# A four-layer decode kernel: two heads' output weights parked in PSUM, parts of two heads of V kept, three units of V read in short transfers

## The chip, the cores and the metric

The kernel runs on 1 core of one Trainium2 chip. Its time is the device time of one execution in microseconds (us), of which the median over several runs is compared. The profile is of one further execution.

## What is computed

Four layers follow each other, attention, a gated block, the same attention again, the same gated block again. The batch is 4 rows with one new position each, the width D is 512, there are 32 query heads over 8 key/value heads of 128, and of the cached 8192 positions the last W = 2048 are attended to.

```python
def _A_ref(x, k_cache, v_cache, wq, wo):
    W = min(4096, max(256, Sk // 4))
    q = (x @ wq).reshape(B, Sq, Hq, Dh).transpose(0, 2, 1, 3)
    k = jnp.repeat(k_cache[:, :, Sk - W:, :], rep, axis=1)
    v = jnp.repeat(v_cache[:, :, Sk - W:, :], rep, axis=1)
    p = softmax(einsum("bhqd,bhkd->bhqk", q, k) * Dh ** -0.5)
    o = einsum("bhqk,bhkd->bhqd", p, v)
    return o.transpose(0, 2, 1, 3).reshape(B, Sq, Hq * Dh) @ wo
def _B_ref(x, w_gate, w_up, w_down):
    return (sigmoid(x @ w_gate) * (x @ w_up)) @ w_down
x = A_x
x = x + _A_ref(_layernorm(x), A_k_cache, A_v_cache, A_wq, A_wo)
x = x + _B_ref(_layernorm(x), B_w_gate, B_w_up, B_w_down)
x = x + _A_ref(_layernorm(x), A_k_cache, A_v_cache, A_wq, A_wo)
x = x + _B_ref(_layernorm(x), B_w_gate, B_w_up, B_w_down)
```

Both attentions use the same K, V, wq and wo, and both gated blocks the same three weights. K and V are 16.8 MB each for the 2048 positions, wq and wo 4.2 MB each, and w_gate, w_up and w_down 1.8 MB each.

## The kernel before

**Storage.** SBUF is cut into units of 256 bf16 columns over 128 partitions, 64 KB each. A head of K or V for the four batch rows is 32 units (2 MB). `kt` has 256 units: all of K, which stays there turned by TensorE from the first attention until the second has used it. `wo_sb` has 64 units, all of wo. `arena` has 75 units, `side` 31; `pt` and `pb` hold weights of the softmax. `WHERE` (lines 426 to 442) names for each load the tensor, the first unit and the number of units. V does not fit beside K, so it is read twice, once in each attention. Half of w_up and w_gate and about half of wq stay from their first use to their second.

**The order of instructions.** Every step is recorded as an operation of a planner with an engine, a planned duration and the blocks and PSUM banks it reads and writes. `_schedule` (line 95) lays the operations out on the engines in advance; `_assign_sync` (line 185) puts the semaphore waits in. All loads but that of x stand on the SyncE queue (SP), strictly in the order in which the program records them: a load that waits until its place is free holds back every load behind it.

**The stages.** First attention: `k_head` turns a head of K (lines 715 to 740), `scores` makes the scores of a head (the matmuls have line 751), the row maximum, the exponential and its transpose; `weights` spreads the result into `pt`; `pv_wo` multiplies by V (line 841 in the wide form, line 883 in the narrow one), scales, and adds the head's share of wo (line 934 for the first seven heads, line 904 for the last). The first gated block is `glu(1, False)`: normalisation, w_up and w_gate (line 1023), w_down (line 1095). `project_q` makes q for the second attention (line 688) from wq, part kept and part loaded as "q01", then subtracts the mean (line 709) and writes `qs` (line 700). The second attention runs the same steps on the K that is still there. V of heads 0 and 1 goes to places in `arena` and `side`; V of heads 2 to 7 goes over K in `kt` as soon as the scores that read that K are done (the load of head h waits for the scores of head h-2). The last gated block is `glu(3, True)`, with w_down in line 1092 and the output copied in line 1105. For the last heads of the second attention `v2_head` (lines 1196 to 1216) adds order edges by hand.

**PSUM.** Eight banks of 2 KB per partition. Banks 0 to 2 take the transposes of K in the first attention, bank 3 its scores, bank 4 sums, banks 5 and 6 the projections and products with V, bank 7 the sum over wo. In the second attention the scores alternate between banks 3 and 0, the turned weights between 1 and 2. `glu` uses banks 0, 1 and 2.

Of the kernel before, what the change touches and what calls it, by code (L numbers as in the profile page):

```python
# [6 lines left out]
BF16 = mybir.dt.bfloat16  # L7
ACTF = mybir.ActivationFunctionType
# [6 lines left out]
class _Op:  # L15
    __slots__ = ("idx", "eng", "name", "dur", "emit", "deps", "odeps", "users", "start", "finish",
                 "sem", "val", "inc", "dma_bytes", "dma_rate", "waits", "prio", "ndeps_left")

    def __init__(self, idx, eng, name, dur, emit):
# [12 lines left out]
        self.inc = 1  # L32
        self.dma_bytes = 0
# [151 lines left out]
def _assign_sync(ops, order, n_dma_sems):  # L185
    counts = {}
    dma_i = 0
    for e in ENGINES:
        for o in order[e]:
            if o.sem is not None:  # L190
                sem = o.sem
            elif e == "sync":
                sem = ("dma", dma_i % n_dma_sems)
                dma_i += 1
                o.inc = 16
            else:
                sem = ("eng", e)
                o.inc = 1
            o.sem = sem
            counts[sem] = counts.get(sem, 0) + o.inc  # L200
            o.val = counts[sem]
# [66 lines left out]
def build(nc, A_x, A_k, A_v, A_wq, A_wo, B_wg, B_wu, B_wd, out):  # L268
# [37 lines left out]
    WIDE = {0: {0: 4, 1: 4, 2: 4, 3: 4, 4: 4, 5: 4, 6: 2}, 2: {2: 2, 3: 2, 4: 2, 5: 2}}  # L306
    HEADS1 = list(range(HKV))
# [29 lines left out]
    with es:  # L337
# [24 lines left out]
        rz = sb("rz", [128, NPT * NR], F32)  # L362
# [40 lines left out]
        def blk_ap(s):  # L403
            return {"kt": kt, "ar": arena, "pt": pt, "pb": pb, "sx": side}[s[0]][:, s[1] * UNIT:(s[1] + s[2]) * UNIT]
# [22 lines left out]
        for h in range(HKV - 1):  # L427
            WHERE["V0_%d" % h] = [ar(MAIN - UHEAD if h % 2 == 0 else 0, UHEAD)]
        WHERE["V0_%d" % (HKV - 1)] = [ar(0, 16), ar(16, 8), ar(24, 8)]
        WHERE["u01"], WHERE["g01"] = ar(MAIN - 2 * GU, 2 * GU), ar(MAIN - 4 * GU, 2 * GU)  # L430
        WHERE.update({
            "g23_1": ar(32, 2 * GU), "u23_1": ar(0, 2 * GU),
            "d0_1": ar(14, 8), "d4_1": ar(22, 8), "d8_1": ar(32, 4), "d10_1": ("pb", 0, 4), "d12_1": ("pt", 4, 4),
            "q01": [ar(36, 10), ar(0, 14), ar(14, 8)],
            "V2_0": [ar(22, 14), sx(0, 8), sx(8, 8), sx(16, 2)],
            "V2_1": [sx(18, NS - 18), ar(0, UHEAD - NS + 18)],
            "g23_3": ar(22, 2 * GU), "u23_3": sx(0, 2 * GU),
            "d0_3": ar(0, 8), "d4_3": ar(8, 8), "d8_3": ar(38, 8), "d12_3": sx(14, 4),
        })
        for h in range(2, HKV):  # L440
            WHERE["V2_%d" % h] = [("kt", (h - 2) * UHEAD + u, n)
                                  for u, n in (((0, 16), (16, 8), (24, 8)) if h == HKV - 1 else ((0, UHEAD),))]
# [20 lines left out]
        def load_v(L, h):  # L463

            got = []
            u0 = 0
            for s in WHERE["V%d_%d" % (L, h)]:
                n = s[2]
                dma("V%d_%d_%d" % (L, h, u0), blk_ap(s), v_d[h][:, :, u0 * UNIT:(u0 + n) * UNIT], w=blk_tok(s),
                    rate={32: "bw_16k", 16: "bw_8k"}.get(n, "bw_4k"), nbytes=128 * n * UNIT * 2)  # L470
                got.append((s, u0 * UNIT // 128))
# [206 lines left out]
        def project_q(L, pieces, pieces_last):  # L678
            if not L:
                return project_first(pieces, pieces_last)  # L680
            prev = []
            toks = []
            wid = NB
            for n, (ap, tk, ktc, q0, q1) in enumerate(pieces):
                def e_q(pe, ap=ap, ktc=ktc, q0=q0, q1=q1, st=(n == 0), last_ktc=pieces_last):
                    last = None
                    for q in range(q0, q1):
                        last = pe.matmul(ps[:, QB, q * wid:(q + 1) * wid],
                                         ap[:, (q - q0) * 128:(q - q0 + 1) * 128],
                                         xn[:, ktc * (NB + 1):ktc * (NB + 1) + wid],  # L690
                                         start=(st and q == q0), stop=(ktc == last_ktc),
                                         skip_group_check=True)
                    return last
                prev = [P.op("tensor", "qproj%d_%d" % (L, n), tm["pe_pair"] * (q1 - q0), e_q,
                             r=list(tk) + [("xn",)], w=[("psq", n)], banks=(QB,), order=prev)]
                toks.append(("psq", n))

            def scaled(src, r, banks):
                P.op("vector", "q_evac%d" % L, c_dve(HQ * NB),
                     lambda v: v.tensor_tensor(  # L700
                         qs[:, 28:28 + HKV * NB * STRIP].rearrange("p (h b s) -> p h b s", h=HKV, b=NB)[:, :, :, 0:REP],
                         src.rearrange("p (h r b) -> p h b r", h=HKV, r=REP)[:, :, 0:NB, :],
                         rstd[:, :].unsqueeze(1).unsqueeze(3).broadcast_to([128, HKV, NB, REP]),
                         ALU.mult),
                     r=r + [("rstd",)], w=[("qs",)], banks=banks)
            if True:
                mc = means(L, tq, cs_q, HQ)
                P.op("vector", "q_mean%d" % L, c_dve(HQ * NB),
                     lambda v: v.tensor_tensor(tq[:, :], ps[:, QB, 0:HQ * NB], tq[:, :], ALU.subtract),
                     r=toks + [mc], w=[mc], banks=(QB,))  # L710
                scaled(tq[:, :], [mc], ())
# [30 lines left out]
        def scores(L, n, h, sbk, tbk):  # L742
# [14 lines left out]
            P.op("tensor", "S%d_%d" % (L, h), 16 * tm["pe_s"] * (0.55 if L == 0 else 1.0), e_s, r=kr + [("qs",)], w=[("pss", sbk)], banks=(sbk,))  # L757
# [32 lines left out]

        def weights(L, n, h, tbk):

            k2 = n % 2
            kp = n % NPT
            ptv = pt[:, kp * NJ4 * NR:(kp + 1) * NJ4 * NR]
            pk = blk_tok(("pt", kp * NR // 4, NR // 4))
# [31 lines left out]
        def wide_pv(L, n, h, wide, bank, out, s):  # L828

            kp = n % NPT  # L830
# [4 lines left out]
            def e_pv(pe):  # L835
                last = None
                for i, (tv, q, c) in enumerate(steps):
                    w0 = (kp * NJ4 + (tv * NB + q) * NCH + c) * NR
# [455 lines left out]
```

## Time and profile before

| what | us |
|---|---|
| median of 3 runs (176.66 to 177.33) | 177.1 |
| the profiled execution, device time | 177.11 |
| its span in the profile | 175.4 |
| TensorE busy in the span | 137.2 |
| VectorE busy | 97.1 |
| ScalarE busy | 71.4 |
| first attention (first instruction to its last wo matmul, line 904) | 0 to 105.6 |
| first gated block, and q | 105.6 to 124.7 |
| second attention (first score matmul to line 904) | 124.7 to 165.1 |
| last gated block | 165.1 to 172.9 |
| output | 172.9 to 175.4 |

The loads move 70.31 MB in 62 transfers, on average 401 GB/s over the span. A busy share of an engine is an average over stages; what a change in a stage is worth shows in which wait of that stage ends last. The times of stages are read from the timeline and the chain of waits. Besides the times of instructions the trace holds a completion record: a wide transfer is shared out to the core's 16 DMA engines, and each adds to the transfer's semaphore when its share has landed, so that a transfer has a first and a last landing.

### The profile page before, as it was taken

Reading aid. Unit: us, or ns where it says so; the run is one execution under the profiler, and the core shown is the slowest. Engines: PE = TensorE matmul, PEld = TensorE weight load, DVE = VectorE, ACT = ScalarE, POOL = GpSimd, SP = SyncE. Lnnn points to the kernel's source line nnn. Section 1 sums busy time; section 2 is a strip of 40 time slices with the busy share of each in tenths; the row PEclk is TensorE's granted clock in tenths of the full one; section 3 lists DMA queues with packets and bytes.
Section 4 is the critical chain, followed back from the end, with each engine's and each line's share of the span. In section 5 each row is a group of like instructions: output and inputs, shape, how many; then the busy total and the mean of one; then the engine's idle time right before and its main releaser. Section 6 shows DMA issues by size and latency. Waiting matters only on the chain.

```text
span 175.4 us, 4862 instructions
## 1 busy us (share of the span) xinstructions
PE 137.2 (78%) x2175; PEld 101.4 (58%) x2175; DVE 97.1 (55%) x240; ACT 71.4 (41%) x125; POOL 6.8 (4%) x17
## 2 busy tenths in 40 slices
PE   0395699898998879988978877449769985978794
PEld 0392488656575657565654567438317753557693
DVE  7444015977848575795884432104298977372440
ACT  2064217848377728384472140300045644341400
POOL 5200000000000000000000002002000000000020
PEclk9999656999999978999999655555586999696858
DMA  5999999999999999999999999999999999999970
GB/s 192 419 424 419 432 441 419 426 419 428 422 419 437 404 441 434 417 426 404 441 422 390 403 420 417 396 403 421 402 427 435 424 426 422 434 405 414 416 285 14
DMA packets 9216, 70.31 MB, mean 401 GB/s; under 512 B 1000, under 2 KB 1772, under 8 KB 5996
## 3 DMA queue, kind: packets, MB, share of 16 engines
q1 hardware_dynamic: 9188, 70.00, 96.1%
q8 instruction: 17, 0.28, 0.6%
q14 instruction: 3, 0.02, 0.0%
q10 hardware_dynamic: 8, 0.00, 0.0%
HBM read 70.00 MB, written 0.00 MB: 399 GB/s over the span
## 4 chain that ended last, share of the span: by engine, by line
DMA 65%; PE 25%; DVE 5%; SPq 2%; ACT 1%; issue 1%; DVEq 0%; ACTq 0%
DMA arena<-in_A_v_cache_dram 31%; DMA kt<-in_A_k_cache_dram 12%; DMA kt<-in_A_v_cache_dram 11%; DMA arena<-in_B_w_down_dram 6%; PE ps L751 5%; DMA arena<-in_A_wq_dram 4%; PE ps L841 4%; PE ps L728 4%; PE ps L883 3%; PE ps L1023 2%; SPq L456 2%; PE ps L821 1%; PE ps L1092 1%; ACT pb L773 1%; DVE nmz L760 1%
## 5 line engine op out<-in xcount | busy, mean ns | idle before, releaser
L738 ACT COPY kt<-ps 128x1024 bf16<-128x1024 bf16 x40 | 39.1, 1017 | 28.0 <-PE ps L728 27.9
L728 PE MATMUL ps<-ident_r,kt 128*128 128x128 bf16 x512 | 40.2, 238 | 5.1 <-DMA kt<-in_A_k_cache_dram 3.2
L728 PEld LDWEIGHTS ps<-ident_r,kt 128*128 128x128 bf16 x512 | 34.7, 109 | 11.9 <-issue 4.4
L738 DVE COPY kt<-ps 128x1024 bf16<-128x1024 bf16 x24 | 29.2, 1215 | 14.1 <-PE ps L728 13.9
L751 PE MATMUL ps<-kt,qs 128*32 128x512 bf16 x256 | 19.2, 429 | 2.5 <-ACT pb L773 1.7
L773 ACT ACTIVATE pb<-ps,nmz 128x512 bf16<-128x512 f32 x16 | 11.1, 691 | 23.6 <-DVE nmz L770 22.1
L806 DVE TENSOR_TENSOR pt<-ps,ofbr 128x1024 bf16<-128x1024 f32 (+1 forms) x16 | 16.2, 1013 | 2.9 <-PE ps L784 2.9
L841 PE MATMUL ps<-arena,pt 128*64 128x512 bf16 (+1 forms) x128 | 13.2, 384 | 3.3 <-DMA arena<-in_A_v_cache_dram 3.3
L760 DVE TENSOR_REDUCE nmz<-ps 128x1 f32<-128x512 f32 x16 | 11.0, 686 | 6.7 <-PE ps L751 6.7
L779 DVE STREAM_TRANSPOSE pb<-pb 128x512 bf16<-128x512 bf16 x16 | 11.2, 700 | 5.1 <-ACT pb L773 5.1
L751 PEld LDWEIGHTS ps<-kt,qs 128*32 128x32 bf16 x256 | 6.0, 103 | 9.8 <-ACT pb L773 2.7
L813 ACT ACTIVATE pt<-ps,ofbr 128x96 bf16<-128x96 f32 x32 | 8.3, 343 | 8.0 <-PE ps L784 8.0
L841 PEld LDWEIGHTS ps<-arena,pt 128*64 128x64 bf16 (+1 forms) x128 | 6.0, 114 | 8.4 <-DMA arena<-in_A_v_cache_dram 4.3
L1023 PE MATMUL ps<-xn,arena 128*128 128x5 bf16 (+1 forms) x196 | 7.4, 172 | 2.6 <-DMA arena<-in_B_w_up_dram 1.1
L1023 PEld LDWEIGHTS ps<-xn,arena 128*128 128x128 bf16 x196 | 7.2, 117 | 2.9 <-DMA arena<-in_B_w_up_dram 1.2
L849 ACT COPY arena<-ps 128x512 f32<-128x512 f32 (+1 forms) x7 | 3.9, 556 | 12.1 <-PE ps L841 12.0
L621 POOL TENSOR_TENSOR rs<-pt,rs 128x4 f32<-128x4 f32 x4 | 4.1, 1014 | 119.7 <-DVE pt L617 119.7
L821 PE MATMUL ps<-rowf,nmz 128*128 128x16 f32 x32 | 7.4, 309 | 1.3 <-DVE pt L806 1.0
L821 PEld LDWEIGHTS ps<-rowf,nmz 128*128 128x128 f32 x32 | 6.0, 233 | 4.1 <-DVE pt L806 1.8
L856 PEld LDWEIGHTS ps<-arena 128*128 128x128 f32 x52 | 6.7, 201 | 2.1 <-ACT arena L849 1.6
L856 PE MATMUL ps<-arena 128*128 128x16 f32 x52 | 7.4, 273 | 0.7
L934 PE MATMUL ps<-wo_sb,onr 128*16 128x512 bf16 x56 | 6.0, 419 | 1.1 <-DVE onr L926 1.1
(127 smaller groups left out, 144.3 us busy)
## 6 DMA issues: line engine op xcount, KB each, us to landing
kt<-in_A_k_cache_dram SPq DMA_DIRECT2D x8, 2048.0 KB, 24.6
arena<-in_A_v_cache_dram SPq DMA_DIRECT2D x7, 2048.0 KB, 20.2
kt<-in_A_v_cache_dram SPq DMA_DIRECT2D x5, 2048.0 KB, 18.5
wo_sb<-in_A_wo_dram SPq DMA_DIRECT2D x8, 512.0 KB, 25.2
arena<-in_B_w_gate_dram SPq DMA_DIRECT2D x3, 896.0 KB, 9.7
arena<-in_B_w_down_dram SPq DMA_DIRECT2D x5, 512.0 KB, 21.6
kt<-in_A_wq_dram SPq DMA_DIRECT2D x1, 2048.0 KB, 11.7
side<-in_A_wq_dram SPq DMA_DIRECT2D x1, 1984.0 KB, 15.9
```

Of the source, the lines that this page charges most:

```text
L728: last = pe.transpose(bankb(bank)[:, (v * NB + q) * 128:(v * NB + q + 1) * 128], kt[:, c0:c0 + 128], ident_b[:, :])
L738: return (e.tensor_copy if ev == "vector" else e.copy)(to, fr)
L751: last = pe.matmul(ps[32 * b:32 * b + 32, sbk, 0:CB * 128], qs[:, q0:q0 + 32], blk_ap(kblk(h, b))[:, c * CB * 128:(c + 1) * CB * 128], sta ...
L760: lambda v: v.tensor_reduce(nmv, ps[:, sbk, 0:CB * 128], AXX, ALU.max, negate=True),
L773: o = a.activation(pbuf[:, :], ps[:, sbk, 0:CB * 128], ACTF.Exp, bias=gv, scale=1.0, accum_out=zv)
L779: P.op("vector", "ptr%d_%d" % (L, h), 650.0, lambda v: v.transpose(turned[:, :], pbuf[:, :]), r=[("pb", 0), ("pb", 1)], w=[("pb", 2), ("pb ...
L806: lambda v: v.tensor_tensor(pv4[:, 0:nj], spread(tbk, nj).unsqueeze(2).broadcast_to([128, nj, NB, REP]), ofb[:, :].unsqueeze(1).unsqueeze( ...
L813: last = a.mul(pv4[:, nj:NJ4, b, :], spread(MB, NJ4 - nj), ofb[:, b:b + 1])
L821: lambda pe: pe.matmul(ps[:, tbk, CB * NQ:CB * NQ + NR], zv.broadcast_to([128, 128]), rowf[:, :], start=True, stop=True),
L841: last = pe.matmul(ps[rows * g:rows * (g + 1), bank, 0:wide * 128].rearrange("p (c d) -> p c d", c=wide), pt[:, w0:w0 + rows], v, start=(i ...
L856: last = pe.matmul(ps[:, out[0], out[1]:out[1] + NR], part[:, c * 128:(c + 1) * 128], ey[wide][:, c * NR:(c + 1) * NR], start=(c == 0), st ...
L1023: last = pe.matmul(ps[:, bank, fc * wid:(fc + 1) * wid], cols[:, fc - g0, :], xn[:, ktc * (NB + 1):ktc * (NB + 1) + wid], start=(ktc == 0 ...
```

## The change

It consists of these parts.

- After the first attention, VectorE copies the output weights of heads 0 and 1 (16 units, 2 MB) bit by bit into PSUM banks 0 to 3 (`stash`), so that 16 units of `wo_sb` are free. During the first gated block and the projection of q they take loads; ScalarE copies the weights back before the second attention uses them. `glu(1)` uses banks 5, 6 and 4 in place of 0, 1 and 2.
- The last 8 units of V of head 6 (in `arena` at 66) and of head 7 (at 24) stay from the first attention; `VKEEP` leaves out their second load. 16 units, 1.05 MB, are not read again. The products with the kept units are made first.
- Many places move. V of head 1 ends and V of heads 2 to 5 starts three units later in `kt`, so that the load of head h now waits for the scores of head h-1. The parts of w_down in the first gated block come in another order.
- `FEW`: the last 2 units of V of head 1 in the first attention, and the last unit of V of head 2 in the second, are loaded by eight transfers each over 16 partitions, which stand ahead of the rest of that head in the queue. On the HBM side each takes 4 positions by 4 batch rows.
- `project_q` puts the first 16 query heads into bank 5 and the others into bank 6, and writes `qs` in two halves: the scores of heads 0 to 3 wait for the first half alone.
- The last head's softmax weights get a third buffer (`PT3`) and its product with V another bank; the hand-made order edges of `v2_head` are gone, and some planned durations differ.

```diff
+    VKEEP = {6: 24, 7: 24}
+    FEW = {(0, 1): 2, (2, 2): 1}
...
-        WHERE["u01"], WHERE["g01"] = ar(MAIN - 2 * GU, 2 * GU), ar(MAIN - 4 * GU, 2 * GU)
+        WHERE["u01"], WHERE["g01"] = ar(52, 2 * GU), ar(38, 2 * GU)
+        PT3 = ar(32, 4)
         WHERE.update({
-            "g23_1": ar(32, 2 * GU), "u23_1": ar(0, 2 * GU),
-            "d0_1": ar(14, 8), "d4_1": ar(22, 8), "d8_1": ar(32, 4), "d10_1": ("pb", 0, 4), "d12_1": ("pt", 4, 4),
-            "q01": [ar(36, 10), ar(0, 14), ar(14, 8)],
-            "V2_0": [ar(22, 14), sx(0, 8), sx(8, 8), sx(16, 2)],
-            "V2_1": [sx(18, NS - 18), ar(0, UHEAD - NS + 18)],
-            "g23_3": ar(22, 2 * GU), "u23_3": sx(0, 2 * GU),
-            "d0_3": ar(0, 8), "d4_3": ar(8, 8), "d8_3": ar(38, 8), "d12_3": sx(14, 4),
+            "g23_1": ("ws", 0, 2 * GU), "u23_1": ar(0, 2 * GU),
+            "d0_1": ar(14, 8), "d4_1": ("ws", 0, 8), "d8_1": ar(32, 4), "d10_1": ("pb", 0, 4), "d12_1": ("pt", 4, 4),
+            "q01": [ar(0, 14), ar(14, 10), ("ws", 8, 8)],
+            "V2_0": [ar(32, 6), sx(0, 16), sx(16, 10)],
+            "V2_1": [sx(26, NS - 26), ar(0, 24), ("kt", 0, 3)],
+            "g23_3": ar(0, 2 * GU), "u23_3": sx(0, 2 * GU),
+            "d0_3": ar(14, 8), "d4_3": ("kt", 179, 8), "d8_3": ("kt", 192, 8), "d12_3": sx(14, 4),
         })
-        for h in range(2, HKV):
-            WHERE["V2_%d" % h] = [("kt", (h - 2) * UHEAD + u, n)
-                                  for u, n in (((0, 16), (16, 8), (24, 8)) if h == HKV - 1 else ((0, UHEAD),))]
+        WHERE["V2_6"] = [("kt", 131, 24), ar(66, 8)]
+        WHERE["V2_7"] = [("kt", 155, 16), ("kt", 171, 8), ar(24, 8)]
+        for h in range(2, HKV - 2):
+            WHERE["V2_%d" % h] = [("kt", (h - 2) * UHEAD + 3, UHEAD)]
...
+            few = FEW.get((L, h), 0)
+            if few:
+                s = WHERE["V%d_%d" % (L, h)][-1]
+                a, m = s[1] + s[2] - few, UHEAD - few
+
+                def e_few(e):
+                    return [e.dma_start(blk_ap((s[0], a, few))[16 * g:16 * g + 16], v_d[h][4 * g:4 * g + 4, :, m * UNIT:UHEAD * UNIT])
+                            for g in range(8)]
+                P.op("sync", "V%d_%d_few" % (L, h), 0.0, e_few, w=blk_tok((s[0], a, few)), dma_bytes=few * UNIT * 256,
+                     dma_rate=tm["bw_1k"]).parts = 8
             for s in WHERE["V%d_%d" % (L, h)]:
...
+                if L == 2 and VKEEP.get(h) == u0:
+                    got.insert(0, (s, u0 * UNIT // 128))
+                    u0 += n
+                    continue
...
+            for i in range(2):
+                tv = tq[:, i * HB * NB:(i + 1) * HB * NB]
+                P.op("vector", "q_mean%d_%d" % (L, i), c_dve(HB * NB),
+                     lambda v, i=i, tv=tv: v.tensor_tensor(tv, ps[:, QB + i, 0:HB * NB], tv, ALU.subtract),
+                     r=toks[i] + [mc], w=[("qm", i)], banks=(QB + i,))
+                P.op("vector", "q_evac%d_%d" % (L, i), c_dve(HB * NB),
...
+                     r=[("qm", i), ("rstd",)], w=[("qs1",)] if i else [("qs",)])
...
+        STASH = ((0, 3), (4, 0), (8, 1), (12, 2))
+
+        def stash(back):
+            for u, b in STASH if back else STASH[1:] + STASH[:1]:
+                at = blk_ap(("ws", u, 4))
+                r, w = [("wo", u * UNIT // WOH)], [("st", b)]
+                if back:
+                    P.op("scalar", "back%d" % u, 1010.0, lambda a, b=b, at=at: a.copy(at, bankb(b)), r=w,
+                         w=r + list(blk_tok(("ws", u, 4))), banks=(b,))
+                else:
+                    P.op("vector", "stash%d" % u, 620.0,
+                         lambda v, b=b, at=at: v.tensor_scalar(ps[:, b, :].bitcast(I32), at.bitcast(I32), 0, None, ALU.bitwise_or),
+                         r=r, w=w + [("pst", b), ("pss", b)] + list(blk_tok(("ws", u, 4))), banks=(b,))
...
+            GB, UB, YB = (0, 1, 2) if last_layer else (QB, QB + 1, MB)
...
-                parts[-2:] = [(8, 10), (10, 12), (12, 14)]
+                parts[1:] = [(10, 12), (12, 14), (4, 8), (8, 10)]
...
+        stash(0)
         glu(1, False)
...
+        stash(1)
         project_q(2, kept_q + streamed, 1)
...
-            if n == HKV - AHEAD - 1:
-                exps[-1].odeps.update(o for o in new if o.name.startswith("pvc"))
...
+            pv_wo(2, n, h, (5, 6), vs2[h], turns[n + 1:n + 2])
```

## The prediction

> **What bounds the kernel.** I first read the slices, then the table by stretches, then the chain of waits, the queue of SP, and the completion record.
>
> ```profile
> span 175.4 us, 4862 instructions
> ...
> PEclk9999656999999978999999655555586999696858
> DMA  5999999999999999999999999999999999999970
> GB/s 192 419 424 419 432 441 419 426 419 428 422 419 437 404 441 434 417 426 404 441 422 390 403 420 417 396 403 421 402 427 435 424 426 422 434 405 414 416 285 14
> ...
> q8 instruction: 17, 0.28, 0.6%
> ...
> DMA 65%; PE 25%; DVE 5%; SPq 2%; ACT 1%; issue 1%; DVEq 0%; ACTq 0%
> ```
>
> All 16 DMA engines are busy from the second slice to slice 38, at 420 GB/s; no compute engine is above 78%. The chain is two thirds DMA.
>
> ```profile
> 112.00:116.00 4.00, 1.66 (x44) 1.49 (x44) 0.52 (x3) 1.22 (x1) 0.00 (x0) 0.50 1.03 387
> 124.00:128.00 4.00, 3.25 (x32) 1.08 (x32) 1.79 (x6) 0.00 (x0) 0.00 (x0) 0.50 1.03 411
> 160.00:164.00 4.00, 3.33 (x89) 2.78 (x86) 1.27 (x4) 1.38 (x2) 0.00 (x0) 0.71 1.02 418
> 168.00:172.00 4.00, 3.90 (x85) 3.42 (x89) 1.20 (x6) 0.25 (x1) 1.01 (x1) 0.50 0.47 180
> ```
>
> Each row is a stretch; the last two columns are the DMA share and GB/s. The share is 1.0 even around q and the gated block: no load ever came too late. After the last load only a tail is left:
>
> ```profile
> 145.01 18.59 DMA kt<-in_A_v_cache_dram
> 163.61 0.05 issue
> 163.65 0.58 PE ps L883 x16
> ...
> 171.12 1.76 PE ps L1092 x54
> ```
>
> The last 8 units of V land at 163.61, and 7.5 us of products and norms follow until w_down starts at 171.12. The last piece of w_down itself lands at 172.19, so that here both ways end within 0.1 us of each other. The time is therefore the bytes, plus whatever holds up the engine that finishes last, plus this tail.
>
> The completion record shows that engine. Head 0 of K lands between 7.74 and 8.38, a spread of 0.64. Each 16 KB fetch of instructions (the q8 row) holds one engine up by 1.2 us: at 24.3 one engine is 1.74 late, by 106 eight are, and at the end the 16 shares land from 168.44 to 172.19: eight engines were hit twice and lie 2.8 to 3.75 behind the first, eight never, within 1.6. A transfer counts when its last share is in, so the hit eight set the time.
>
> **The bytes.** 16 units of V are not read: 16 x 64 KB / 16 = 64 KB per engine. A packet of 16 KB takes 612 ns in the trace, so 4 x 0.612 = 2.45 us less on every engine.
>
> **The short transfers, bytes.** Three units leave the wide transfers: 12 KB per engine, 0.46 us less. Where do they go? The output transfer has the same shape (16 partitions, 4 by 4 rows in HBM), and its record has four landings in place of 16; so has that of x, over 4 partitions. I take it that four engines, always the same, carry all three units: 32 packets of 1 KB at 46 ns (the 640 such packets) and 32 of 512 B at 27 ns, 1.5 + 0.9 = 2.4, net 1.9 more on these four. If they are among the eight that are never hit, they end at most 1.6 + 2.4 behind where the others now gain 0.46, about level with the late ones; the sum on the late engines is then -2.45 - 0.46 = -2.9 us. Which four, the record doesn't name. The nine engines whose first packet of K takes 0.63 to 0.75 (seven take 1.0 or more) hold the five that lead later and are not hit by the first eight fetches; the four that had just moved x are probably among them. The other answer is rival C.
>
> The Trainium skill, page "DMA: Bandwidth & Descriptors", section on why a DMA increments its semaphore by 16, states that a transfer runs on the largest number of engines, up to 16, that divides the slowest dimension of both sides, and on the lowest-numbered ones; by that rule it is four, engines 0 to 3, and the four landings of the output agree.
>
> **The queue of SP.** Here the cover matters, and it is thin in one place only. Before, at each issue, I compared its end with the first landing of the transfer ahead. The lead is 12 us and more in the first attention, 1.8 to 3.6 in the gated block and q, 3.0 at V of head 2, then 6 to 13.
>
> ```profile
> 123.91 0.54 SPq L456 DMA_DIRECT2D arena<-in_A_v_cache_dram  x1
> 126.69 18.92 SPq L456 DMA_DIRECT2D kt<-in_A_v_cache_dram  x8
> ...
> 173.22 0.69 SPq L456 DMA_DIRECT2D out_dram<-pb  x1
> ...
> 121.33 1.58 PE L688 MATMUL ps<-xn,arena 128*128 128x4 bf16 x50
> 123.29 0.59 PE L688 MATMUL ps<-xn,arena 128*128 128x4 bf16 x16 [0.38 <-DMA arena<-in_A_wq_dram]
> 124.75 3.58 PE L751 MATMUL ps<-kt,qs 128*32 128x512 bf16 x32 [0.86 <-DVE qs L700]
> ```
>
> The first eight short transfers (V of head 1, at 9 us) cost SP 5 us or, if the queue is full, some 20; the load behind the last one issued there is waited for only at 38, and what is in flight reaches past 50: nothing. The wide loads keep their leads in the gated block on the late engines (3 us and more); only early engines may pause, which costs nothing.
>
> The second eight stand ahead of V of head 2, which now waits for the scores of head 1, not of head 0. Scores of head 1 end: the second piece of q01 brings the same 24 units as before, at 121.96 - 0.3; then 20 matmuls (50 take 1.58) 0.7, to 122.35; half of the two DVE steps (0.87 with gaps for the whole) 0.65, to 123.0; the two heads of scores at the granted clock of 0.5 took 1.94 and 1.69: 126.65. Before, this load was issued at 126.69, so the split of q pays for the later head. But now SP first issues eight short ones. Price: a load of a weight takes 0.33 (plus 0.04 gap), one of V 0.53 to 0.60, the output 0.69. I take V's 0.605 + 0.045, the same direction and pattern: 5.2 us (3.0 to 6.4 by the others). V of head 2 is issued at 131.85, and a first packet comes 1.3 to 1.45 after an issue starts (output, first K): 133.25.
>
> What is ahead of it ends, less the 0.3 of the first short ones, at 129.6 on the first engine and 132.5 on the last (landings 130.24 and 133.19; data end 0.35 before). So every engine runs dry, the early ones for over 3 us, the last for 0.75, and all start level. From the landing of V of head 1 to the end the first engine needed 168.44 - 130.24 = 38.2, now less 17 units (2.6): 35.6. So 133.25 + 0.35 + 35.6 = 169.2, and the five fetches still to come hit five different engines once: 170.4, against 172.19: -1.8. Likewise the last V: 26.9 in place of 29.5, 161.65 against 163.61: -1.95. Without the pause it would be -2.9; the point from which the pause decides is a first packet at 132.1.
>
> **The tail.** The last 24 units of V come in one head's 3.7 us instead of 5.1 for 32. Between the landing of head 6 and its wo matmul lie 48 narrow products (1.5 at half clock), scaling, selection and wo, with gaps 3.1; then `pb` (0.59), its remainder (0.69), the turn (0.35) and wo of head 7 (0.57) in PE's order: 1.85 after the last landing, 1.46 before. +0.4 on the chain through compute: -1.95 + 0.4 = -1.55.
>
> **The rest**, at nothing. `stash`: four copies of 128x512 at some 0.69 (line 953's row) on DVE, which waits 1.67 and 2.02 us in two places of that stretch; the load that needs the room has a lead of 5.3. `back`: four ACT copies of 1.02 (line 738's row); two come before, two after the last piece of q and ahead of the first exponential, which is about 1 us later; the loads that wait for later scores have leads of 6 and more. PV of the last head of the first attention comes 0.55 later behind the turn; the product that follows waits 0.64 for its weight anyway. New places and the third buffer move no bytes.
>
> **Sum**: 177.11 (profiled; the median is 177.1) - 1.55 = **175.6 us**.
>
> **Rivals.**
>
> B, the cover holds: the short issues cost as little as a weight's (3.0), or the clock is granted earlier and the scores take 1.05 each as at 129.06, so that V of head 2 comes by 132.1. For it: the clock was full from 128.2. Against: V's pattern has three dimensions and 0.53 is its least. Then -2.9 + 0.4: 174.6.
>
> C, the four engines are among the hit ones. Late by 3 us already at V of head 1, they carry 1.4 - 0.3 and 0.9 more, end at 134.8, 1.6 after the start of the others: -1.55 + 1.6, about 177.2. Against it the first packets above.
>
> D, the slower one: short transfers don't follow each other without a gap on their four engines. The output's shares have landed 0.46 after its first packet. If each of the 16 holds its engines for that long, each eight take 3.7. Engines never hit end V of head 1 by 130.3 (0.7 behind the first) + 3.7 - 0.3 = 133.7, and the second eight by 137.4, later than the pause of the others. Their last V lands at 137.4 + 0.35 + 26.9 = 164.6, which is +1.0, with the tail's 0.4 +1.4: 178.5. It decides from 0.37 us each, where they would start V of head 2 at 136. Against: wo's 1 KB packets follow each other at 46 ns.
>
> The Trainium skill, same page, section "Rules for kernel authors", speaks against the change here: transfers under 64 KB are mostly overhead and should be joined; these are 16 and 8 KB. Its section "Measured" gives 0.68 us for 4 KB, by which 16 would take 10.9 us and the time, an estimate, would be some 182. No row here shows such a sequence.
>
> **Chances.** Forecast 0.45, with issue prices between those of V and of the output giving 175.0 to 176.8; B 0.28, C 0.15, D 0.12. Range 174.3 to 177.3: it leaves out most of D and the edge of B. A measurement can tell 0.5%, 0.9 us: faster is below 176.2. That is B and three quarters of the forecast, 0.62; C and the rest are no change, 0.26; slower 0.12.
>
> **What would show it.** Right: 69.3 MB; eight issues at about 126.7 and V of head 2 near 132; a dip of the DMA share around 130 to 133; the landings of V of head 2 close together, against 2.97 apart before; last V near 161.7. B shows no dip and a spread above 2 us; C and D the short units landing with or after everything else on four engines. A dip in another stage, above all in the gated block, would make the forecast wrong, as would a compute wait there on `stash` or `back`.

## The result, and the profile after

| | median, us | range | ratio to before, 95% interval |
|---|---|---|---|
| before | 177.00 (6 runs) | 176.66 to 177.93 | |
| changed kernel | 179.44 (6 runs) | 179.07 to 180.34 | 1.0133 (1.0109 to 1.0157) |

The change makes the kernel slower by 1.3%, where 175.6 us was forecast. Some executions fall into a slower state, so medians and ratios, here and below, are of the others alone. The profiled execution after took 180.34 us, the slowest of its six and 0.9 above their median; its span is 178.6 against 175.4. The page of the changed kernel, with the lines that were read first before:

```profile
span 178.6 us, 4888 instructions
...
PEclk9999759999879999999999555555587969955555
DMA  5999999999999999999999999999987999999960
GB/s 210 433 411 415 429 437 418 426 405 370 419 429 433 405 432 427 418 429 414 417 435 386 411 418 422 376 326 382 405 342 281 409 422 433 408 379 415 415 261 6
...
DMA 47%; PE 25%; SPq 16%; DVE 7%; issue 2%; ACT 1%; DVEq 0%
```

The row of DMA shares shows one dip (the 8 and 7, about 130 to 138 us). The row of GB/s shows two: 376, 326, 382 between 112 and 125 us, where the share is still 9, and 342, 281 at the place of the dip. SP's queue is 16% of the chain of waits, 2% before. The table by stretches of the changed kernel (last two columns: DMA share, GB/s):

```profile
112.00:116.00 4.00, 1.69 (x50) 1.52 (x48) 0.81 (x5) 1.53 (x2) 0.00 (x0) 0.50 1.04 379
116.00:120.00 4.00, 2.51 (x73) 2.16 (x71) 0.74 (x5) 1.28 (x2) 0.00 (x0) 0.50 1.03 344
120.00:124.00 4.00, 3.02 (x94) 2.85 (x91) 1.21 (x7) 0.74 (x1) 1.01 (x1) 0.50 1.00 348
124.00:128.00 4.00, 3.23 (x41) 1.51 (x41) 1.41 (x4) 2.02 (x2) 0.00 (x0) 0.50 0.99 410
...
132.00:136.00 4.00, 3.49 (x83) 2.33 (x83) 3.53 (x10) 2.20 (x8) 0.00 (x0) 0.64 0.54 186
```

Before, the same five moved 387, 413, 410, 411 and 436 GB/s. From 112 to 132 us, 0.66 MB less is moved than before, 1.6 us at 420 GB/s; from 132 to 140 another 1.1 MB. SP's issues in the timeline of the changed kernel tell why (start, duration, what is loaded):

```profile
105.97 0.43 SPq L462 DMA_DIRECT2D pt<-in_B_w_down_dram  x1
112.30 0.33 SPq L462 DMA_DIRECT2D wo_sb<-in_B_w_down_dram  x1
112.67 0.43 SPq L462 DMA_DIRECT2D arena<-in_B_w_down_dram  x1
114.48 2.11 SPq L462 DMA_DIRECT2D arena<-in_A_wq_dram  x2
...
128.74 5.35 SPq L479 DMA_DIRECT2D kt<-in_A_v_cache_dram  x8
134.13 1.86 SPq L462 DMA_DIRECT2D kt<-in_A_v_cache_dram  x3
```

`d4` goes to the room of the first output weights, where w_gate's second half lies until its last product; so it is issued at 112.30, not at 104.68. Behind it in the queue stand `d8`, whose place has long been free, and q's weights. The lead (first landing of the load ahead, less the end of the issue) is 0.9 us at `d4` and 1.3 at q's first piece; before, none in the gated block and q was under 1.8. Then the eight short issues hold V of head 2 until 134.13. The chain of waits of the changed kernel (start, duration, what) goes through both places, and from there through compute to the end:

```profile
105.12 10.47 DMA arena<-in_B_w_down_dram
...
116.26 7.32 DMA arena<-in_A_wq_dram
...
125.10 3.60 PE ps L771 x32
...
134.13 8.70 DMA kt<-in_A_v_cache_dram
142.83 0.14 issue
142.97 1.60 PE ps L864 x32
...
166.06 1.39 PE ps L907 x48
167.45 0.12 issue
167.57 0.36 PE ps L985 x8
167.92 0.44 PE ps L929 x16
```

In the completion record the last V lands at 165.26 (before 163.61) and w_down at 174.28 (172.19). The last wo matmul ends at 168.36, 3.1 us after the last V; before it was 1.46.

### The profile page after: what moved, and what is told of

Its sections match the earlier page's. It is cut to its first block, busy times and chain, and to the rows that moved or that the text cites. A ratio compares the mean times of both kernels' runs of the same rounds, so it can differ in the third digit from the quotient of the medians.

```text
span 178.6 us, 4888 instructions
## 1 busy us (share of the span) xinstructions
PE 139.1 (78%) x2175; PEld 101.9 (57%) x2175; DVE 99.0 (55%) x246; ACT 75.3 (42%) x129; POOL 6.8 (4%) x17
## 4 chain that ended last, share of the span: by engine, by line
DMA 47%; PE 25%; SPq 16%; DVE 7%; issue 2%; ACT 1%; DVEq 0%
DMA arena<-in_A_v_cache_dram 32%; SPq L479 11%; PE ps L864 7%; DMA arena<-in_B_w_down_dram 6%; DMA kt<-in_A_v_cache_dram 5%; SPq L462 4%; PE ps L771 4%; DMA arena<-in_A_wq_dram 4%; PE ps L907 2%; PE ps L1062 2%; DVE pt L829 2%; PE ps L748 2%; PE ps L879 1%; PE ps L844 1%; DVE nmz L780 1%
## 5 line engine op out<-in xcount | busy, mean ns | idle before, releaser
L748 PE MATMUL ps<-ident_r,kt 128*128 128x128 bf16 x512 | 39.3, 234 | 4.5 <-DMA kt<-in_A_k_cache_dram 2.3
L748 PEld LDWEIGHTS ps<-ident_r,kt 128*128 128x128 bf16 x512 | 33.4, 106 | 11.9 <-issue 4.6
L864 PE MATMUL ps<-arena,pt 128*64 128x512 bf16 (+1 forms) x128 | 14.3, 390 | 4.4 <-DMA arena<-in_A_v_cache_dram 4.4
L829 DVE TENSOR_TENSOR pt<-ps,ofbr 128x1024 bf16<-128x1024 f32 (+1 forms) x15 | 15.4, 1028 | 1.0 <-PE ps L804 0.9
L864 PEld LDWEIGHTS ps<-arena,pt 128*64 128x64 bf16 (+1 forms) x128 | 6.5, 112 | 9.5 <-DMA arena<-in_A_v_cache_dram 3.1
L836 ACT ACTIVATE pt<-ps,ofbr 128x96 bf16<-128x96 f32 x28 | 7.2, 342 | 7.6 <-PE ps L804 6.1
L1062 PE MATMUL ps<-xn,arena 128*128 128x5 bf16 (+1 forms) x168 | 6.3, 172 | 2.0 <-DMA arena<-in_B_w_up_dram 1.1
L1002 ACT COPY wo_sb<-ps 128x1024 bf16<-128x1024 bf16 x4 | 4.0, 1012 | 8.7 <-PE ps L1135 4.5
L864 PE MATMUL ps<-kt,pt 128*32 128x256 bf16 x128 | 5.6, 332 | 2.6 <-DMA kt<-in_A_v_cache_dram 2.6
```

The costliest lines, as they stand in the source:

```text
L748: last = pe.transpose(bankb(bank)[:, (v * NB + q) * 128:(v * NB + q + 1) * 128], kt[:, c0:c0 + 128], ident_b[:, :])
L829: lambda v: v.tensor_tensor(pv4[:, 0:nj], spread(tbk, nj).unsqueeze(2).broadcast_to([128, nj, NB, REP]), ofb[:, :].unsqueeze(1).unsqueeze( ...
L864: last = pe.matmul(ps[rows * g:rows * (g + 1), bank, 0:wide * 128].rearrange("p (c d) -> p c d", c=wide), ptv[:, w0:w0 + rows], v, start=( ...
L1062: last = pe.matmul(ps[:, bank, fc * wid:(fc + 1) * wid], cols[:, fc - g0, :], xn[:, ktc * (NB + 1):ktc * (NB + 1) + wid], start=(ktc == 0 ...
```

## The experiments

Three theories were weighed. P: the eight short issues ahead of V of head 2. G: late issues in the gated block and q, which starve the engines. T: the compute chain at the end of the second attention. Each ratio is to the kernel before, run on the same chip.

| kernel | median, us | ratio, 95% interval |
|---|---|---|
| e1 no short transfers | 177.17 | 1.0020 (0.9986 to 1.0055) |
| e2 first eight only | 177.54 | 1.0032 (1.0002 to 1.0061) |
| e3 second eight only | 179.58 | 1.0152 (1.0123 to 1.0180) |
| e4 second eight behind V of head 2 | 178.36 | 1.0079 (1.0046 to 1.0112) |
| e5 before, 16 units not read | 176.30 | 0.9953 (0.9926 to 0.9980) |
| e6 e1, hand-made order at the end | 179.02 | 1.0124 (1.0050 to 1.0198) |
| e7 e1, loads reordered | 175.84 | 0.9932 (0.9898 to 0.9965) |
| e8 e1, 16 units read again | 180.32 | 1.0175 (1.0106 to 1.0244) |
| e13 loads of e1, compute order of e7 | 177.14 | 0.9987 (0.9964 to 1.0010) |
| e14 loads of e7, compute order of e1 | 176.41 | 0.9961 (0.9940 to 0.9981) |
| e9 e7 with both sets of short ones | 180.75 | 1.0182 (1.0156 to 1.0207) |
| e10 e7, one wide transfer for the second set | 176.47 | 0.9964 (0.9940 to 0.9988) |
| e15 before, four later waits | 177.66 | 1.0045 (1.0021 to 1.0069) |
| e11 e7, two loads cut in two | 176.17 | 0.9962 (0.9942 to 0.9983) |
| e12 e7 with the first eight | 177.45 | 1.0023 (0.9996 to 1.0049) |
| e16 e7, 8 units kept | 177.34 | 1.0027 (1.0000 to 1.0054) |

### The short transfers: e1 to e4

```diff
-    FEW = {(0, 1): 2, (2, 2): 1}
+    FEW = {}                  # e1
+    FEW = {(0, 1): 2}         # e2
+    FEW = {(2, 2): 1}         # e3
```

In e4 both sets stay, and the second is recorded after the wide load of V of head 2.

> The changed kernel with no short transfers at all: the three units go back into the wide loads of V (0.46 us more on most engines). Theory P (the eight issues ahead of V of head 2 are the main loss: SP issues them from 128.74 to 134.09, and the engines run dry): V of head 2 is issued near 128.8, the low stretch at 132 to 136 us is gone, and the time is 175.0 to 176.0. Theory G (most was lost before, in the gated block and the projection of q, where the share of DMA also falls): only some 1.5 us come back, 177.5 to 178.5, and the scores of head 1 still end near 128.5. Theory T (the products of the second attention are what is late at the end): the last units of V land 3 us earlier but the time falls by less than 2, to 177.5 or more.

> The changed kernel with only the first eight short transfers (two units of V of head 1, first attention). If these cost nothing, as forecast, the time is that of the kernel with no short ones, less up to 0.3. If the four engines that carry them are late from then on (four landings of V of head 1 came 1.6 us later than before, and w_up some 0.9), it is 0.5 to 1.5 us above it, and the loads of the first gated block are issued later by as much.

> The changed kernel with only the second eight short transfers (one unit of V of head 2, second attention). Theory P: near the changed kernel itself, 178.5 to 179.5, and 3 us or more above the kernel with no short ones. Theory G: within 1.5 us of the kernel with no short ones. If the first eight are what makes the gated block late, the scores of head 1 end near 127 here and the time is some 1.5 under the changed kernel.

> The changed kernel with both sets, the second one issued behind the wide load of V of head 2 in place of ahead of it: same bytes, same four engines, same number of issues, only their place in the queue of SP. Theory P: V of head 2 is issued near 128.8, the low stretch at 132 to 136 us is gone, and the time falls by 2.5 to 3.5 us, to 176 to 177. If it is the bytes on four engines or gaps between short transfers that cost, it stays at 179.

The second eight cost 1.0% (changed kernel against e2) to 1.3% (e3 against e1), 1.8 to 2.3 us; the first eight cost nothing here that can be measured (e2 against e1). Moving the second eight behind the wide load takes back 0.5%, 1.0 us, about half of their price and less than the 2.5 to 3.5 expected. In e4's profile, which is of its fastest execution, that load is issued at 128.38 and there is no hole behind it (422 and 433 GB/s from 128 to 136 us), but its runs spread from 176.9 to 179.1; the load of V of head 3, now held up in turn, has a lead of 2.6. What the other half is was not taken apart: the short transfers still keep their four engines. So P is right, and it is not the whole: with no short transfer at all the kernel stands where it was before, not at 175 to 176. Against the kernel before, nothing is left there of the 16 units that are not read. e1's table by stretches:

```profile
116.00:120.00 4.00, 2.51 (x77) 2.17 (x74) 0.88 (x5) 1.64 (x2) 0.00 (x0) 0.50 1.00 362
120.00:124.00 4.00, 3.12 (x90) 2.80 (x90) 1.55 (x8) 1.06 (x2) 1.01 (x1) 0.50 0.95 334
124.00:128.00 4.00, 3.82 (x49) 1.58 (x42) 1.99 (x6) 2.13 (x4) 0.00 (x0) 0.50 0.97 362
128.00:132.00 4.00, 2.58 (x28) 1.10 (x32) 3.43 (x11) 1.80 (x6) 0.00 (x0) 0.85 1.03 370
```

From 112 to 132 us (with 388 in the first stretch) it moves 0.96 MB less than before, 2.3 us of transfer: about the 2.45 us that were saved.

### What the bytes and the moves are worth alone: e5, e8

```diff
                 n = s[2]
+                if L == 2 and h >= HKV - 2 and u0 == 24:     # e5, on the kernel before
+                    got.insert(0, (s, u0 * UNIT // 128))
+                    continue
...
-    VKEEP = {6: 24, 7: 24}
+    VKEEP = {}                                               # e8, on e1
```

> The kernel before with one edit: the last 8 units of V of heads 6 and 7 are not loaded in the second attention, and their products, made first in each head, take what lies in their place (K of heads 4 and 5), so that the output is not the reference's. No output weight is moved, no place changes, no transfer is short. If the byte term of the forecast holds where nothing else is touched (16 units, 2.45 us on every engine, and the compute chain behind the last V follows), the time is 174.4 to 175.0. If the products of the last heads can't follow so early, it stays at 175.5 or more.

> The kernel with no short transfers, but with the 16 units of V read again into their places in the second attention: all the moves of the change without its saving. Theory G (the transfers set the end, and the gated block gives the saving back): 2.45 us above the kernel with no short ones, 179.3 to 179.8. Theory T (the compute chain of the second attention sets the end there, and the saved bytes are hidden behind it): only 0.4 to 0.9 us above it, 177.6 to 178.1.

e8 is 1.55% above e1, 2.7 us, which the intervals leave at 1.4 to 4.1: in the moved kernel the saved bytes are worth their price. T's expectation for e8 fails. e5 is worth less than expected: 0.5%, 0.8 us. In its profile the transfers gain what was forecast (w_down lands at 169.63, 2.56 earlier, the last V 2.63 earlier), and so does the last wo matmul (it ends at 162.66, 2.42 earlier), but the output is issued only 1.28 earlier. Its chain of waits, from the last wo matmul on:

```profile
162.25 0.41 PE ps L909 x16
...
162.92 0.64 PE ps L1028 x15
163.56 1.14 issue
164.69 0.57 PE ps L1028 x13
```

TensorE stands still for 1.14 us in the middle of the products with w_up, for which the profile shows no wait; what it waits for stayed open. This pause is what the output is short of in this profile: up to the last wo matmul compute follows the transfers, even though nothing is moved. The price of all the moves together can be read twice: without the 16 units, e1 against e5, it is 0.67% or 1.2 us; with them, e8 against the kernel before, it is 1.75% or 3.1 us (1.06 to 2.44%). Why the two differ was not settled.

### The order of the loads: e7, e13, e14

```diff
-                parts[1:] = [(10, 12), (12, 14), (4, 8), (8, 10)]
+                parts[1:] = [(10, 12), (12, 14), (8, 10), (4, 8)]
-            "q01": [ar(0, 14), ar(14, 10), ("ws", 8, 8)],
+            "q01": [("ws", 8, 8), ar(0, 14), ar(14, 10)],
```

> The kernel with no short transfers, with two changes of order in the gated block and q: the part of w_down that waits for nothing late goes ahead of the part that waits for the products with w_gate, and the piece of q's weights that goes to the freed room of the output weights is loaded first, the one that waits for the products with w_up behind it. Theory G (issues that come with a lead of only 1.1 to 1.7 us starve the engines between 112 and 132 us; 2.3 us of transfer are lost there against the kernel before): the moved data from 112 to 124 us come nearer to the 410 GB/s of before, V of head 2 lands 0.5 to 1 us earlier than 139.92, and the time falls to 176.2 to 176.8. If the engines are slow there for another reason than late issues: no gain in the GB/s of these stretches and 177.0 or more.

e7 is the fastest kernel of this study, 0.7% under the one before. From 112 to 124 us its transfers come nearer to those of before:

```profile
112.00:116.00 4.00, 1.86 (x52) 1.72 (x52) 0.52 (x3) 1.14 (x1) 0.00 (x0) 0.50 1.06 396
116.00:120.00 4.00, 2.34 (x70) 2.00 (x67) 0.88 (x5) 1.05 (x2) 0.00 (x0) 0.50 0.99 404
120.00:124.00 4.00, 2.70 (x82) 2.53 (x79) 1.06 (x6) 2.90 (x3) 1.01 (x1) 0.50 0.98 378
```

V of head 2 lands at 138.48, 1.44 earlier than in e1, where 0.5 to 1 was expected. (The profile of e1 is of an execution 0.7 us above its median, that of e7 of one 0.7 below, so the two lie further apart than the medians.) Its SP timeline: `d8` goes out at 106.09, and behind `d4` there is a load that can go at once.

```profile
106.09 0.43 SPq L462 DMA_DIRECT2D arena<-in_B_w_down_dram  x1
111.26 0.33 SPq L462 DMA_DIRECT2D wo_sb<-in_B_w_down_dram  x1
111.63 0.43 SPq L462 DMA_DIRECT2D wo_sb<-in_A_wq_dram  x1
113.46 1.62 SPq L462 DMA_DIRECT2D arena<-in_A_wq_dram  x2
```

The planner, though, had also put operations of the second attention in another order (products of heads 3 and 5 earlier). e13 and e14 cross the two, by order edges that pin the engines' order from the scores of head 2 on:

```diff
+        for e, names in PIN.items():
...
+            for o, p in zip(chain[1:], chain):
+                if p not in o.deps:
+                    o.odeps.add(p)
```

> The reordered loads of the gated block made the time 175.84, but the planner had also put some operations of the second attention in another order (the products of heads 3 and 5 earlier). Here the loads are those of the kernel with no short transfers (177.17), and the order of TensorE, VectorE and ScalarE from the scores of head 2 on is that of the reordered kernel. Theory G (late issues of loads in the gated block): 177.0 to 177.4, no gain. Theory O (the planner's order of the second attention is what gained): 175.6 to 176.2.

> The counterpart: the reordered loads of the gated block, with the three engines' order from the scores of head 2 on as in the kernel with no short transfers. Theory G: 175.6 to 176.2. Theory O: 177.0 to 177.4. Both in part: between, and the two kernels' differences from 177.17 add up to the 1.33 us.

In ratios, the loads are worth 0.59% with the old order (e1 to e14) and 0.55% with the new (e13 to e7), about 1.0 us; the order of compute 0.33% and 0.29%, some 0.5 us, which is within the intervals. (That either pair adds up to e7's 0.88% follows from how they are formed.) So the loads are the larger part of e7's gain; that the order of compute has a part is not shown.

### Late waits put into the kernel before: e15

```diff
+        by = dict((o.name, o) for o in P.ops)
+        for load, late in (("wd1_8", "glu_g1_3"), ("wq2_0", "glu_u1_3"), ("wq2_10", "glu_d1_0"), ("V2_0_14", "qproj2_1")):
+            by[load].deps.add(by[late])
```

> The kernel before, with four waits added and nothing else: its loads of w_down (part 8), of q's first and second piece and of the second piece of V of head 0 wait for the products that the changed kernel's loads wait for (w_gate's last, w_up's last, w_down's first part, q's second kept piece). Same bytes, same places, same order on every engine. Theory G (late issues are what costs in the gated block): the moved data between 112 and 128 us fall below 390 GB/s and the time rises by 0.8 to 1.8 us, 178.0 to 179.0. If the moves themselves (other places, copies, banks) cost it: no change, 177.0 to 177.4.

```profile
112.00:116.00 4.00, 1.65 (x44) 1.49 (x44) 0.52 (x3) 1.11 (x1) 0.00 (x0) 0.50 1.00 375
116.00:120.00 4.00, 2.88 (x84) 2.56 (x85) 0.91 (x6) 0.00 (x0) 0.00 (x0) 0.50 0.99 373
120.00:124.00 4.00, 2.97 (x85) 2.71 (x83) 1.02 (x6) 0.00 (x0) 1.01 (x1) 0.50 1.01 357
```

With the same bytes, places and engine order, four later issues alone take 0.45% (0.21 to 0.69), 0.7 us in the median; w_down lands 0.9 later, and V of head 2 at 139.92, as in e1, against 138.09 before. From w_down's part 8 to q's second piece the leads are 0.7 to 1.6 us; the load of V of head 0 keeps 3.5. The size is a little below what was expected. From 112 to 124 us, against the kernel before, 0.56 MB less is moved in the changed kernel, 0.50 in e1, 0.42 in e15 and 0.13 in e7. So late issues alone can bring most of that loss. The other 0.46 MB that e1 lacks are missing from 124 to 132 us (362 and 370 GB/s against 411 and 435), where e15 loses none (418 and 445). By the medians, late issues make more than half of the moves' price if that is 1.2 us, a quarter if it is 3.1, and never all.

### Order edges at the end: e6

```diff
...
+                mine[1].odeps.add(named["sel2_%d" % HEADS2[n - 1]])
+                named["WO2_%d" % HEADS2[n - 1]].odeps.add(mine[1])
+                mine[2].odeps.add(named["WO2_%d" % HEADS2[n - 1]])
...
```

The other edges of the kernel before (the copy of head 5's product ahead of the last exponential, and three more) are put back as they were.

> The kernel with no short transfers (177.2), with order edges for the last heads put back: the product of head 5 ahead of the last exponential, 16 and 32 products of head 7 between the scaling of head 6 and its wo matmul, so that only 16 are left behind it. Theory T (TensorE's order is what is late at the end: 3.35 us from the landing of the last V to the end of wo of head 7, against 1.46 before): 175.2 to 176.0, and the last wo matmul ends within 1.9 us of that landing. Theory G (the lost transfer time of the gated block alone sets the end): no change, 176.9 to 177.4.

It is slower by 1.0% instead, so the missing edges are not the loss. Why it is slower was not settled: in its profile V of head 2 also lands 1.25 later than in e1. Where compute is late in e1's profile can be read from the stretches behind V of head 2, first e1, then e7 (the third column from the end is TensorE's granted clock, 1.00 being full speed):

```profile
140.00:144.00 4.00, 4.00 (x54) 2.28 (x58) 1.05 (x3) 0.63 (x3) 0.00 (x0) 0.50 1.01 434
144.00:148.00 4.00, 4.00 (x56) 2.40 (x52) 3.05 (x9) 1.81 (x6) 0.00 (x0) 0.72 0.98 414
```

```profile
140.00:144.00 4.00, 3.80 (x72) 2.40 (x71) 3.07 (x9) 2.21 (x9) 0.00 (x0) 1.00 1.01 426
144.00:148.00 4.00, 3.60 (x70) 2.44 (x73) 3.49 (x11) 2.37 (x10) 0.00 (x0) 1.00 1.01 426
```

In e1 TensorE waited 1.45 us for V of head 2 and then worked without a gap at half clock; from there to the end e1's chain of waits holds no transfer any more. In e7 it has the full clock there, and the chain goes through the load of V of head 6 until 157.43. Why the clock fell was not isolated: a wait alone doesn't bring it, since e15's TensorE waited 2.15 us for V of head 4, until 149.68, and kept the full clock to 155. So T holds in a part: in e1 and in the changed kernel, once V of head 2 is late, compute sets the end.

### The eight issues again, and what else could be had: e9 to e12, e16

e9 and e12 are e7 with both sets and with the first set. e10 reads the same unit by one issue:

```diff
-                    return [e.dma_start(blk_ap((s[0], a, few))[16 * g:16 * g + 16], v_d[h][4 * g:4 * g + 4, :, m * UNIT:UHEAD * UNIT])
-                            for g in range(8)]
+                    return e.dma_start(blk_ap((s[0], a, few)), v_d[h][:, :, m * UNIT:UHEAD * UNIT])
...
```

> The changed kernel itself with the reordered loads of the gated block and nothing else edited: both sets of short transfers are in. If their price (179.44 against 177.17, 2.3 us) stands by itself: 175.84 + 2.3, 177.6 to 178.6. If it came from the thin cover that the late loads left, it shrinks: below 177.0.

> The kernel with reordered loads (175.84), with the last unit of V of head 2 taken out of the wide load and read ahead of it by one transfer over 128 partitions, where the change has eight over 16. Theory P (the price is SP's time for eight issues, 5.35 us): one issue of 0.55 to 0.65 us fits under the lead of 2.3 us, and the time is 175.6 to 176.4. If the split of the load or the unit's own packets cost it: 177.5 or more.

> The kernel with reordered loads (175.84) with the first eight short transfers alone (V of head 1, first attention). It gives their price where the second set doesn't stand behind them: 175.8 to 176.4 if it is the 0.5 us that the kernel without reordered loads showed, 175.6 if the forecast's nothing is right, 177 or more if they also make the loads of the gated block late.

e9 is slower than the changed kernel. The reordered loads give up the early half of q, so the eight issues begin at 129.54 and V of head 2 goes out at 134.93; this stretch of e9 shows the hole that it leaves:

```profile
132.00:136.00 4.00, 3.11 (x52) 1.80 (x53) 3.37 (x10) 2.00 (x9) 0.00 (x0) 0.69 0.19 68
```

One issue in their place (e10) has 0.3% over e7, within the intervals; so it is the eight short transfers that cost (1.6%, e9 against e12), not the cut of the load. e10 changes both the number of issues and the number of engines that carry the unit, so it doesn't tell these two apart; the hole, in which all 16 engines together have a share of 0.19, is the wait for SP. The first set costs 0.9% over e7 here and nothing measurable in e2, though e12 moves 393 to 405 GB/s from 112 to 124 us, in sum no less than e7. The planner's order in the first attention differs in the kernels that have it; this stays open.

e11 cuts the second load of V of head 0 and the one of head 1 in two, so that the first halves can go earlier. e16 keeps only V of head 7's 8 units, and uses the other 8 as an early room for V of head 0.

> The kernel with reordered loads (175.84), with two loads cut in two, so that the first halves need not wait for the rooms of the second: 16 units of V of head 0 (its issue had a lead of only 0.5 us) and 24 of V of head 1 (1.8 us). Theory G: another 0.2 to 0.7 us, 175.1 to 175.6. If the rest of the loss lies in the compute chain of the second attention: 175.7 to 176.2.

> The kernel with reordered loads (175.84), keeping 8 units of V (head 7) in place of 16; the 8 units that come free take the second piece of V of head 0, whose load then need not wait for the projection of q. Theory G: the pause at 121 to 125 us is gone (about 0.6 to 1 us) and 8 units more are read (1.2 us), of which part is hidden behind the compute chain: 175.6 to 176.4. If keeping 16 units is worth its whole 2.45 us: 177.0.

Neither gains: e11 is 0.3% and e16 0.95% above e7. So nothing more is shown to be had at these two issues, and it is better to keep both.

## Why the prediction was wrong

**The step that failed** is "The wide loads keep their leads in the gated block on the late engines (3 us and more); only early engines may pause, which costs nothing." It was priced at nothing. The leads of the kernel before were read correctly in the gated block and q (in the first attention, "12 us and more" leaves out the last loads of V, which have 7.9 and 3.2), but the moves change what each load waits for: `d4` for w_gate's last product, q's first piece for w_up's. Leads of 0.9 to 1.3 us to the first engine were left. It is true that the early engines pause first: in e1 the landings are 3.4 us apart at w_down's first part and 2.4 at q's last piece, which ends as early as before (123.30, 123.25). But it doesn't cost nothing: the last landing is 0.4 us behind that of before at the end of V of head 0, 1.4 at head 1 and 1.8 at head 2 (139.92), where TensorE waits for it, and e15, which adds nothing but the waits, is 1.8 behind there too and 0.7 us slower in the median. The moves cost 1.2 us (e1 against e5) or more.

How the pause of the early engines reaches the late ones is open in part: 1.0 of e1's 1.8 us is lost in one load, the 5-unit piece of V of head 1, which was issued 4.3 us ahead. Its last landing comes 1.79 us after that of the load ahead, in e7 0.78.

**The pause at V of head 2** was right in mechanism and in price: 5.35 us for the eight issues, 5.2 was taken; all engines level afterwards (landings 1.8 us apart, forecast close together). Its start was 2.05 late: the scores of head 1 end at 128.70, not 126.65, since q's second piece landed at 123.58, not 121.66. That is the failed step again, one stage on, and the first short transfers have a part in it: without them, in e3, the eight issues begin at 127.85, with them at 128.74. So V of head 2 went out at 134.13, not 131.85, and the second set was worth 1.8 to 2.3 us where 1.1 was counted for the pause (from -2.9 to -1.8).

**The bytes** were right for the transfers (2.56 us earlier in e5, 2.45 counted), and nearly so to the end of the second attention, where e5's last wo matmul ends 2.42 earlier. What was mis-sized is the term behind it, that the output follows the last V with 0.4 more: in e5's profile it came 1.28 us earlier, not 2.2, because of the pause of 1.14 us in the last gated block, whose cause is open; in the medians e5 gains 0.8. In the changed kernel the last wo matmul ends 3.1 us after the last V, 1.86 was forecast: there compute, and no transfer, stands in the chain from 142.97 on.

Of the 3.8 us between forecast and result, the moves make 1.2 (e1 against e5), the second set 0.7 to 1.2 more than counted, and the saved bytes 1.2 less (0.8 in place of 2.45 - 0.4). The rest is not assigned.

**At nothing**: the first eight short transfers don't show in the time of e2, though w_up lands 1.0 us later in the changed kernel than in e3; in e12 they show with 0.9%. `stash` and `back` were not taken out alone, so their price stays open. They move 16 units, which is 1.05 MB, not the 2 MB that the description of the change gives.

**The rivals.** B fell: the cover did not hold. C's sign is there, w_up's last landing 0.94 later than before, but e2 gives no price for it. D, the slower one, has the right side, and its gaps are there: on their four engines the last of the first eight lands 1.9 to 2.8 us after the first, seven transfers further, which is 0.34 each in the mean, where four 1 KB packets without a gap would take 0.18. That is just under the 0.37 from which D decides, and e4, with the same transfers in another place, was 0.5% below the changed kernel. So the forecast's 2.4 us for both sets on these engines were too low, but what held V of head 2 in the changed kernel was SP, which issued without a pause until 134.09.

The short transfers' record has four landings each, and the rest of the 16 counts at once when SP issues it. That is what the Trainium skill, page "DMA: Bandwidth & Descriptors", section on why a DMA increments its semaphore by 16, says of a transfer that uses four engines. Its 0.68 us for 4 KB (section "Measured") is for transfers over 128 partitions issued from GpSimd, so it was no price for this row from SP: 16 KB each took 0.34.

The prediction itself named the test: "A dip in another stage, above all in the gated block, would make the forecast wrong." The dip is there, in the row of GB/s and not in the row of shares, from which the prediction had read that "no load ever came too late".

## What to carry to other kernels

When loads get new places, list for each what it now waits for and what stands behind it in the queue, and work out the lead anew: one late load in an in-order queue takes the lead of all behind it. Put a load that can go at once ahead of one that must wait; here two swaps in the order took the kernel without short transfers from level with the one before to 0.7% under it. A row of issues costs its queue the sum of their times, which must fit under what is in flight at that point.

## What the runs showed of the hardware that was not expected

- A DMA share near 1.0 doesn't mean full speed: in e1 the share is 0.95 to 1.03 at 334 to 370 GB/s (116 to 132 us). The share counts the recorded time of packets, and that can grow: the 2560-byte packets of V of head 1 took a median of 211 ns in e1 and 102 in the changed kernel and in e7. Why in e1 nearly all of them are slow was not settled; their load had been issued 4.3 us ahead.
- Beside the first eight short transfers other packets are slower: from 40.0 to 43.2 us in the changed kernel the 15360-byte packets took a median of 0.70 us, from 43.2 to 47 us 0.58. That the short transfers cause it was not tested; the few ahead of 40 us had 0.66.
- The bytes don't decide what an issue costs SP: 0.62 to 0.67 us for 8 KB over 16 partitions, 0.54 for 64 KB over 128 (e10) and 0.53 for 2 MB, all of V, but 0.33 for 0.9 MB of w_up.
